# One core of a Trainium2 chip: a new hand-written order for the first layer norm and transform of a spectral block with a gated feed-forward, with its loads cut differently

## The chip, the cores and the metric

The kernel runs on one core of a Trainium2 chip. The time is device microseconds of one execution, taken as the median of several runs; smaller is better. Besides the time there is one profiled execution, whose trace shows every instruction of the engines: PE (TensorE matmul) with PEld (its weight loads), DVE (VectorE), ACT (ScalarE), POOL (GpSimd) and SP (SyncE, which here only issues DMAs). Times inside the trace are microseconds from the start of its span.

## The reference

```python
def A(x, w_r, w_i):                      # spectral filter over (2048 tokens, 576 features)
    X = rfft2(x.astype(float32)) * (w_r + 1j * w_i)
    return irfft2(X, s=(2048, 576)).astype(bfloat16)
def B(x, w_gate, w_up, w_down):          # 576 -> 4608 -> 576
    return (gelu(x @ w_gate) * (x @ w_up)) @ w_down
h   = x + A(layernorm(x))
out = h + B(layernorm(h))
```

All inputs are bfloat16, with 2048 tokens of 576 features, and the layer norms have no parameters.

## The kernel before

The 2048 tokens are held as 16 tiles of 128 partitions (token 16p + c is partition p of tile c), each 576 wide, in `XO`. The kernel has four stages, all in one program whose instructions are recorded in order and given to the engines as one queue each; an engine runs its queue strictly in order, and semaphore waits are derived from what each operation reads and writes.

**Front (L484 to L585).** For each tile a mean and variance is formed: on DVE by two `bn_stats` of half a tile each (L496) and one `bn_aggr` (L505), or, for the three tiles named by a `Q` token, on ACT by a sum (`S`, L488) and a sum of squares (`Q`, L492), after which POOL squares the mean (`m`, L499) and DVE forms the variance (L508). The 16 tiles go in six groups, of 2, 2, 3, 3, 3 and 3 tiles. For each group ACT takes a square root (`q`, L512), DVE a reciprocal (`c`, L517), and the transform table `ATB` is scaled by it into `ATS` (`x`: on POOL one instruction for a group, L522; on DVE one for each tile, L527). POOL also negates a part of the tiles into `XN` (`n`, L569) and copies 64 tail columns of each tile into it (`t`, L574). The token transform `M` (`a_mm`, L553) of a group is five positions of 2 matmuls for each tile; each position writes a PSUM bank of its own, and the banks go round in eights, so that a position of a later group waits until an earlier position's bank has been emptied. Emptying is the eviction `E` (L564, on ACT or DVE) into `U`. Evictions whose number appears in an `F` token are split: `E` moves the half of the columns that the first half of the next stage reads, and `F` moves the rest later. `k` puts matmuls on zeros into the PE queue.

The order of all of this is written out by hand in the string `SEQ1` (L25): each word is an operation, its group, tile or eviction number, and, with A, D or P behind it, the engine. `M3`, for example, is the transform of group 3, and `E18D` eviction number 18 on DVE. Eviction number n belongs to group n // 5.

**D stage (SEQF, about 20 to 43.6 us).** For 16 frequency groups: feature transform D (L642), B (L662), multiplication T by the filter on DVE (L675), V (L683), with evictions on ACT and DVE (L608). The filter lies in `WS`. SP loads it from HBM in many small pieces (`w_up`, `w_down`, `w_zero`); two of the `w_down` pieces are issued by POOL. Then `WS` is duplicated on the other partitions by `dup_w`: piece 0 by two POOL instructions (L732, behind the last `x`) and two DVE instructions (L730), and pieces 1 to 3 by DMAs that POOL issues. T of group i reads the duplicate 0 for i below 5, 1 from 5, 2 from 8, and 3 from 12 on.

**Inverse transform (SEQ)** with the residual add and the second layer norm, to about 55.5 us; loads of the first gate and up weights are held back on SP until given matmuls. **Feed-forward**: four blocks of 512 tokens, each 36 gate and up products (L946) and the down product (L1046, L1058).

The load order of the front is `LORD` (L26): `x4-8` is one DMA with tiles 4 to 7 of the input, and `a4-8` one with those tiles' tables. They go out on SP in that order, ahead of the tables `FT` and `BT`, the filter pieces and `VT`.

Of the kernel before, what the change touches and what calls it, by code (L numbers as in the profile page):

```python
# [7 lines left out]
ALU = mybir.AluOpType  # L8
# [12 lines left out]
NPRE = 8  # L21
PARTS = ((0, 256), (256, 512))
GROUPS = ((0, 2), (2, 4), (4, 7), (7, 10), (10, 13), (13, 16))
SEQ1 = """B0 b0 S3 B2 Q3 n0 B1 b1 b2 n1 t0 m3P t2 v0 v1 n2 t1 q0 c0 k14 x0D q1 M0 E0A S4 m4P c1 x1D n3 E2A k104 b5 t3 b7 Q4 E1A M1 E7A B5 B6 E8A b6 B7 v2 q2 B11 E5A B8 c2 x2P E3A E9A b8 b9 B9 v3 E6A n4 B12 Q13 E4A k206 M2 b10 q3 c3 b11 S13 x3P E11A B10 t4 b12 v4 E10A B14 m13P E14A M3 q4 c4 x4P E12A E13A t5 b14 E15A b15 B15 v5 E16A E18D E17A q5 M4 E20A E19A E23A c5 x5D n5 E24A F24D F23D E21A M5 E25A E26D E22A E28D E27A E29D F25A F29D F26A F27A F28A F22A""".split()
LORD = "x0-2 x2-4 a0-4 x4-8 a4-8 x8-12 x12-16 a8-16".split()  # L25
SPLIT = tuple(int(w[1:-1]) for w in SEQ1 if w[0] == "F")  # L26
ACT_TILES = tuple(int(w[1:]) for w in SEQ1 if w[0] == "Q")
SEQF = """D2 D0 d2 D1 d0 d1 B2 D5 B0 d5 T2 D3 B1 d3 D4 T0 T1 B5 d4 D8 B3 d8 D7 T3 B4 d7 V0 D6 v0 V1 T5 d6 v1 R0 V2 r0 v2 T4 B6 D9 B8 T6 V3 d9 D11 v3 d11 B7 D10 B9 d10 V6 V4 T7 v6 v4 V5 B10 v5 R1 D12 T8 r1 d12 B11 T9 V7 D14 v7 T10 d14 D13 B12 d13 D15 T11 V9 T12 d15 v9 V8 B13 v8 R2 r2 T13 B14 T14 B15 V12 V10 v12 v10 V13 V11 T15 v13 V14 v11 v14 V15 R3 v15 r3""".split()
# [9 lines left out]
def _np_bf16(a):  # L38
    npdt = mybir.dt.np(BF16)
    return np.ascontiguousarray(np.asarray(a, dtype=np.float32).astype(npdt))  # L40
# [291 lines left out]
def _build(nc, A_x, A_w_r, A_w_i, B_w_gate, B_w_up, B_w_down, out):  # L332
    P = Prog(nc)
    T = build_tables()
    dram = {n: nc.inline_tensor(_np_bf16(T[n]), name="c_" + n.lower()) for n in T}
    PE, DVE, ACT, SP, POOL = "pe", "dve", "act", "sp", "pool"
# [4 lines left out]
    XO = sb.alloc("XO", [128, NT, D], BF16)  # L341
# [19 lines left out]
    XN = sb.alloc("XN", [128, NT, 448], BF16)  # L361
# [27 lines left out]
    BT = sb.alloc("BT", [128, 2, 2, 128], BF16)  # L389
    VT = sb.alloc("VT", [128, 6, 2, 128], BF16)  # L390
# [32 lines left out]
    def bank(b, p0=0, p1=128, c0=0, c1=512):  # L423
        return PS[p0:p1, b * 512 + c0:b * 512 + c1]
# [18 lines left out]

    for i, w in enumerate(LORD):
        (x_load if w[0] == "x" else atb_load)(i, int(w[1:].split("-")[0]), int(w.split("-")[1]))
    P.dma(SP, FT[:, :, :].rearrange("p a b -> p (a b)"), dram["FTAB"][:, :], "ft", w=["FT"])
    P.dma(SP, BT[:, 0, :, :].rearrange("p b c -> p (b c)"), dram["BTAB"][:, 0:256], "bt", w=["BT"])

    def w_up(pl, hf):
        g0, g1 = ((0, 9), (9, 16))[hf]  # L450
# [5 lines left out]
    def w_down(pl, hf, sls=(0, 1, 2, 3), eng=SP, sem=""):  # L456
        g0, g1 = ((1, 9), (9, 16))[hf]
        src = (A_w_r, A_w_i)[pl].tensor
        for sl in sls:
            p0 = 64 * (sl // 2) + 32  # L460
            P.dma(eng, WS[p0 + sl % 2:p0 + 32:2, sl // 2, pl, g0:g1, :], bass.AP(src, (64 + 16 * (3 - sl) + 16 - g0) * K2, [[128 * K2, 16], [-K2, g1 - g0], [1, K2]]),
                  f"w{pl}{hf}{sem}", w=[("W", hf, pl, 2 + sl)])

    def w_zero(pl):
        for jp in range(2):
            P.dma(SP, WS[64 * jp + 32:64 * jp + 64, jp, pl, 0, :], bass.AP((A_w_r, A_w_i)[pl].tensor, (64 + 32 * jp) * K2, [[128 * K2, 16], [(-16 if jp else 48) * K2, 2], [1, K2]]),
                  f"wz{pl}", w=[("W", 2, pl, jp)])

    for pl in (1, 0):
        w_up(pl, 0)  # L470
        w_down(pl, 0)
    P.dma(SP, VT[:, 0, :, :].rearrange("p b c -> p (b c)"), dram["VTAB"][:, 0:256], "vt", w=["VT"])
    for pl in (1, 0):
        w_up(pl, 1)
        w_down(pl, 1, (0, 1, 2, 3) if pl else (0, 1))
    for pl in (1, 0):
        w_zero(pl)
    P.dma(SP, VT[:, 1, :, :].rearrange("p b c -> p (b c)"), dram["VTAB"][:, 256:512], "vt1", w=["VT1"])
    P.dma(SP, BT[:, 1, :, :].rearrange("p b c -> p (b c)"), dram["BTAB"][:, 256:512], "bt1", w=["BT1"])
    GORD = list(range(1, NG)) + [0]  # L480
    wkeys = [[("W", hf, pl, h) for pl in range(2) for h in range(6 if hf < 2 else 2)] for hf in range(3)]

# [47 lines left out]
    AORD = (1, 0, 3, 2, 4)  # L530

    def a_bank(i, k):
        return (5 * i + AORD.index(k) + ABASE) % 8

    def idle_mm(a):
        b = a_bank(a // 100, AORD[0])
        for _ in range(a % 100):
            P.op(PE, lambda t: t.matmul(bank(b), ZD[:, 0:128], ZD[:, :], start=True, stop=True), r=["ZD"], w=[("PS", b)])  # L538

# [24 lines left out]
        fn = (lambda v: v.tensor_copy(dst, src)) if eng == DVE else (lambda a: a.activation(dst, src, ACTF.Copy))  # L564
        P.op(eng, fn, r=[("PS", b)] + ([("EV", n)] if late else []), w=[("U", i, k, h) for h in hs] + ([] if late else [("EV", n)]))

    def x_neg(i):
        c0, c1 = GROUPS[i]
        P.op(POOL, lambda g: g.tensor_scalar(XN[:, c0:c1, 0:256], XO[:, c0:c1, 288:544], -1.0, 1.0, op0=ALU.mult, op1=ALU.mult),  # L569
             r=[("X", c) for c in range(c0, c1)], w=[("XN", c) for c in range(c0, c1)])  # L570

    def x_tail(i):
        c0, c1 = GROUPS[i]
        P.op(POOL, lambda g: g.tensor_scalar(XN[:, c0:c1, 320:384].rearrange("p c (a e) -> p c a e", a=2),  # L574
                                             XO[:, c0:c1, :].rearrange("p c (a e) -> p c a e", a=2)[:, :, :, 256:288], 1.0, 1.0, op0=ALU.mult, op1=ALU.mult),
             r=[("X", c) for c in range(c0, c1)], w=[("XT", c) for c in range(c0, c1)])

    P.op(DVE, lambda v: v.memset(XN[:, :, 256:448].rearrange("p c (a e) -> p c a e", e=64)[:, :, 0::2, :], 0.0), w=["XZ"])

    ENG = {"A": ACT, "D": DVE, "P": POOL}  # L580
    RUN1 = {"k": idle_mm, "S": act_sum, "Q": act_sq, "B": lambda c: ln1_half(c, 0), "b": lambda c: ln1_half(c, 1), "v": ln1_var, "q": ln1_sqrt, "c": ln1_rs, "M": a_mm, "x": ln1_scale, "E": a_ev, "F": lambda n, eng: a_ev(n, eng, True), "n": x_neg, "t": x_tail, "m": act_mean2}
    P.op(ACT, lambda a: a.activation(SA[:, 0, 0:1], EPT[:, 0:1], ACTF.Sqrt), r=["EPT"], w=[("SA0", 0)])
    for w in SEQ1:
        a = w[1:]
# [9 lines left out]
    for t, w in enumerate(SEQF):  # L594
        k, i = w[0], w[1:].rstrip("abc")
        if k in "DBVR":
            b = min((b for b in used if b not in busy), key=lambda b: used[b])
# [4 lines left out]
        elif k in "dvr":  # L602
            b = FB[k.upper(), int(i)]
# [117 lines left out]
    def dup_w(k, jp, pl=slice(0, 2), eng=None):  # L721
        a, b = 64 * jp, 64 - 64 * jp
        n = ("Wd", k, jp, pl.start)
        for g0, g1 in (((1, 6),), ((6, 9),), ((9, 13),), ((13, 16), (0, 1)))[k]:
            dst, src = (WS[q:q + 64, jp, pl, g0:g1, :].rearrange("p a g k -> p a (g k)")[:, :, 1:] for q in (b, a))
            r = [x for x in (wkeys[1] if g0 > 8 else wkeys[0] if g0 else wkeys[0] + wkeys[2]) if pl.start <= x[2] < pl.stop]
            if eng is None:
                op = P.dma(POOL, dst, src, f"wd{k}{jp}", r=r, w=[(*n, g0)])
            elif eng == DVE:
                P.op(DVE, lambda v: v.tensor_copy(dst, src), r=r, w=[(*n, g0)])  # L730
            else:
                P.op(POOL, lambda v: v.tensor_scalar(dst, src, 1.0, 1.0, op0=ALU.mult, op1=ALU.mult), r=r + [("ATS", NT - 1)], w=[(*n, g0)])  # L732
        return op if eng is None else None

    for jp in range(2):
        dup_w(0, jp, slice(1, 2), POOL)
        dup_w(0, jp, slice(0, 1), DVE)
    for jp in range(2):
        dup_w(1, jp)
    w_down(0, 1, (2, 3), POOL, "p")  # L740
    c = 0
    while c < NT:
        c1 = c + 1
# [5 lines left out]
        c = c1  # L749
# [34 lines left out]
    for w in SEQF:  # L784
        i = int(w[1:].rstrip("abc"))
# [26 lines left out]
    for t, w in enumerate(SEQ):  # L812
        k, i = w[0], int(w[1:].rstrip("ADSP"))
        if k in "INu":
            b = min((b for b in range(2 * ing, 4) if b not in held), key=lambda b: last[b])
# [3 lines left out]
        elif k in "ioUEae":  # L819
            b = SLOT[{"i": "I", "o": "N", "U": "u", "E": "I", "a": "N", "e": "u"}[k], i] // 2  # L820
# [145 lines left out]
    for w in SEQ:  # L966
        a = w[1:]
# [132 lines left out]
def bass_sequential_preLN__spectral_gfnet__geglu_ffn__prompt_kernel(  # L1100
    nc, A_x, A_w_r, A_w_i, B_x, B_w_gate, B_w_up, B_w_down, out
):
    _build(nc, A_x, A_w_r, A_w_i, B_w_gate, B_w_up, B_w_down, out)
# [28 lines left out]
```

## Time and profile before

| what | us |
|---|---|
| median of 3 runs (lowest, highest) | 486.07 (485.85, 486.44) |
| the profiled execution's own time | 485.97 |
| its span in the trace | 484.2 |
| PE busy | 477.5 (99%) |
| DVE, ACT, POOL busy | 183.3, 146.3, 52.2 |
| first transform matmul (M0), first D matmul | 7.08, 19.91 |
| end of the D stage's chain, first gate matmul | 43.6, 55.47 |
| granted TensorE clock | 1.00 in every stretch asked for |

The span is the trace's first to last instruction; the profiled execution took 1.77 us more than that. A timeline row gives the start, the duration, the engine, the line, the operation, and `out<-in` with the number of instructions in it; a duration of several instructions runs from the first one's start to the last one's end, and instructions of one engine overlap a little, so the distance from start to start ("pitch") is what one costs in a row of them.

### The profile page before, as it was taken

How to read it: one execution, taken by the hardware profiler on the slowest of the kernel's cores; microseconds unless marked ns; L12 is line 12 of the kernel's file. 1: busy time of each engine (PE TensorE's matmuls, PEld its weight loads, DVE VectorE, ACT ScalarE, POOL GpSimd, SP SyncE). 2: the span in 40 equal slices, each digit the busy share in tenths (PEclk: the TensorE clock that was granted, in tenths of full speed). 3: DMA queues.
4: the chain of work that ended last, by engine and by line, in shares of the span. 5: the costliest groups of instructions: out<-in, count | busy, mean ns of one | idle time of the engine just before them, and what ended most of it. 6: DMA issues, size and time to landing. Idle time of an engine off the chain costs nothing.

```text
span 484.2 us, 12895 instructions
## 1 busy us (share of the span) xinstructions
PE 477.5 (99%) x5875; PEld 304.4 (63%) x5876; DVE 183.3 (38%) x366; ACT 146.3 (30%) x295; POOL 52.2 (11%) x88
## 2 busy tenths in 40 slices
PE   8999999999999999999999999999999999999998
PEld 4877765555588744444688644444788544445884
DVE  7898755665500144333200234333101233333011
ACT  6998753434300032233100132223100133223000
POOL 6873317010120000000000000000000000000000
DMA  8865889941430001000000011000000000000000
GB/s 283 215 142 160 251 279 282 374 109 27 173 100 27 26 15 23 20 1 0 3 14 15 26 24 23 13 1 1 3 14 27 14 1 1 0 1 1 3 26 26
DMA packets 28582, 33.19 MB, mean 69 GB/s; under 512 B 12640, under 2 KB 21872, under 8 KB 28528
## 3 DMA queue, kind: packets, MB, share of 16 engines
q1 hardware_dynamic: 24864, 19.87, 14.3%
q0 software_dynamic: 3664, 12.50, 8.1%
q8 instruction: 46, 0.75, 0.7%
q14 instruction: 8, 0.07, 0.1%
HBM read 26.21 MB, written 2.36 MB: 59 GB/s over the span
## 4 chain that ended last, share of the span: by engine, by line
PE 95%; DMA 1%; DVE 1%; POOL 1%; SPq 0%; issue 0%; POOLq 0%; DVEq 0%
PE PS L946 58%; PE PS L1046 27%; PE PS L642 2%; PE PS L1058 2%; PE PS L683 2%; DMA XO<-in_A_x_dram 1%; PE PS L553 1%; PE PS L662 1%; PE PS L837 1%; PE PS L996 1%; DVE XO L860 1%; SPq L242 0%; PE PS L1013 0%; PE PS L854 0%; POOL XN L569 0%
## 5 line engine op out<-in xcount | busy, mean ns | idle before, releaser
L946 PE MATMUL PS<-HT,WG 64*128 64x512 bf16 (+1 forms) x2142 | 233.5, 373 | 0.1
L946 PEld LDWEIGHTS PS<-HT,WG 64*128 64x128 bf16 x2142 | 116.1, 94 | 104.4 <-DVE AT L955 0.2
L954 ACT ACTIVATE GL<-PS 128x512 bf16<-128x512 f32 x144 | 85.7, 596 | 281.7 <-PE PS L946 281.7
L955 DVE TENSOR_TENSOR AT<-GL,PS 128x512 bf16<-128x512 bf16 x144 | 98.8, 687 | 166.0 <-ACT GL L954 166.0
L1046 PE MATMUL PS<-WD,AT 64*128 64x288 bf16 x2160 | 133.0, 283 | 0.0
L1046 PEld LDWEIGHTS PS<-WD,AT 64*128 64x128 bf16 x2160 | 114.3, 94 | 18.7
L1033 DVE TENSOR_TENSOR OS<-PS,XO 128x288 bf16<-128x288 f32 (+2 forms) x32 | 13.2, 452 | 125.5 <-PE PS L1046 118.0
L946 PE MATMUL PS<-HT,WGX 64*128 64x512 bf16 x486 | 53.5, 376 | 0.0
L946 PEld LDWEIGHTS PS<-HT,WGX 64*128 64x128 bf16 x486 | 25.7, 94 | 26.7
L863 ACT ACTIVATE OS<-XO,NM 128x576 bf16<-128x576 bf16 x15 | 11.6, 773 | 11.4 <-DVE XO L1017 11.4
L642 PE MATMUL PS<-FT,U 64*128 64x288 bf16 x160 | 13.3, 283 | 0.0
L675 DVE TENSOR_TENSOR TP<-YS,WS 128x1024 bf16<-128x1024 bf16 x16 | 11.0, 686 | 0.4 <-PE PS L683 0.2
L564 ACT ACTIVATE U<-PS 128x384 bf16<-128x384 f32 (+2 forms) x31 | 10.5, 427 | 1.2 <-PE PS L553 1.1
L496 DVE BATCH_NORM_STATS2 ST<-XO 128x6 f32<-128x288 bf16 x26 | 10.0, 441 | 1.8 <-DMA XO<-in_A_x_dram 1.8
L242 POOL DMA_DIRECT2D WG<-in_B_w_gate_dram x9 | 6.1, 679 | 35.5 <-DMA WG<-in_B_w_gate_dram 32.1
L683 PE MATMUL PS<-VT,TP 64*128 64x128 bf16 x256 | 9.9, 217 | 0.0
L553 PE MATMUL PS<-ATS,XO 128*128 128x128 bf16 x96 | 8.2, 220 | 1.5 <-POOL ATS L522 0.8
L242 POOL DMA_DIRECT2D WD<-in_B_w_down_dram x9 | 6.7, 756 | 22.9 <-PE PS L1013 22.9
L608 ACT ACTIVATE CUS<-PS 128x576 bf16<-128x576 f32 x14 | 9.1, 656 | 0.4 <-PE PS L642 0.2
L1058 PE MATMUL PS<-WD,AT 128*128 128x448 bf16 (+1 forms) x72 | 9.0, 286 | 0.0
L538 PE MATMUL PS<-ZD 128*128 128x512 bf16 x23 | 7.5, 484 | 1.5 <-POOL ZD L431 1.5
L608 ACT ACTIVATE YS<-PS 128x576 bf16<-128x576 f32 x14 | 8.8, 653 | 0.1
(88 smaller groups left out, 231.3 us busy)
## 6 DMA issues: line engine op xcount, KB each, us to landing
WD<-in_B_w_down_dram POOLq DMA_DIRECT2D x9, 576.0 KB, 13.0
WG<-in_B_w_up_dram SPq DMA_DIRECT2D x6, 576.0 KB, 6.6
WG<-in_B_w_gate_dram POOLq DMA_DIRECT2D x6, 576.0 KB, 6.2
out_dram<-OS SPq DMA_DIRECT2D x30, 72.0 KB, 1.7
XO<-in_A_x_dram SPq DMA_DIRECT2D x3, 576.0 KB, 7.1
WGX<-in_B_w_up_dram SPq DMA_DIRECT2D x2, 576.0 KB, 4.5
WGX<-in_B_w_gate_dram POOLq DMA_DIRECT2D x2, 576.0 KB, 5.8
HT<-HN SPq DMA_TRANSPOSE x60, 2.4
```

What stands on the lines that cost most here:

```text
L242: fn = lambda e: e.dma_start(out_ap, in_ap)
L553: P.op(PE, lambda t, b=b, lhs=lhs, p0=p0, p1=p1, s=s, e=e, o=o, c=c: t.matmul(bank(b, p0, p1, o, o + 128), lhs, ATS[:, c, :], start=s, sto ...
L608: fn = (lambda v: v.tensor_copy(dst, src)) if eng == DVE else (lambda a: a.activation(dst, src, ACTF.Copy))
L642: return P.op(PE, lambda t: t.matmul(bank(b0 + o, 0, 128, 0, 2 * HK), U[64 * h:64 * h + 64, us, 2 * i:2 * i + 2, :, :], FT[64 * h:64 * h + ...
L683: return P.op(PE, lambda t: t.matmul(bank(b0 + o, 0, 128, 128 * c, 128 * c + 128), TP[64 * h:64 * h + 64, z, o, t_, c:256:2], VT[64 * h:64 ...
L863: P.op(ACT, lambda a, c=c, out=out: a.activation(out, XO[:, c, 0:D], ACTF.Square, bias=NM[:, c:c + 1], accum_out=SB2[:, 1, c:c + 1]), r=[( ...
L946: op = P.op(PE, lambda t, h0=h0, kt=kt, wt=wt, b=b, s=(not second and j == 0), e=(second and j == n - 1): t.matmul(bank(b, 0, 128, c0, c1) ...
L954: P.op(ACT, lambda a: a.activation(GL[:, s2, :], bank(b0), ACTF.Gelu_apprx_tanh), r=[("PS", b0)], w=[("GL", s2)])
L955: P.op(DVE, lambda v: v.tensor_tensor(AT[:, f, :], GL[:, s2, :], bank(b0 + 1), op=ALU.mult), r=[("GL", s2), ("PS", b0 + 1)], w=[("AT", f)])
L1033: P.op(DVE, lambda v: v.tensor_tensor(OS[:, p % 2, d0:d1], bank(b, 0, 128, 0, d1 - d0), XO[:, c, d0:d1], op=ALU.add), r=[("PS", b), ("X", ...
L1046: e[h] = P.op(PE, lambda t, f=f, h=h, r0=r0, j=j: t.matmul(bank(b0 + h, 0, 128, 0, 288), AT[r0:r0 + 64, f, 128 * p:128 * p + 128], WD[r0:r ...
L1058: P.op(PE, lambda t, b=b, d0=d0, d1=d1, f=f, j=j: t.matmul(bank(b, 0, 128, 0, d1 - d0), AT[:, f, 128 * p:128 * p + 128], WD[:, f, d0:d1], ...
```

## The change

- `LORD`: the tiles 4 to 11 come in four pieces of two tiles where two pieces of four stood; the tables 4 to 15 come as one piece, between tiles 8-12's second half and tiles 12-16, where they came as two pieces, `a4-8` after tiles 4-8 and `a8-16` last of all. SP issues nine loads where it issued eight.
- `BT` and the first third of `VT` are loaded whole in one DMA each; the two late DMAs with their second parts are gone from SP.
- `SEQ1` is another order. The tiles with statistics on ACT are 2, 7 and 10 (before 3, 4 and 13). The scaling `x` of groups 0 and 1 is on POOL (before DVE). The tail copies `t2`, `t4` and `t5` are on DVE (before POOL). Four evictions are split (22, 27, 28, 29; before 22 to 29). DVE has the evictions 18, 20, 24 and 25, the first halves 27 and the second halves 27 and 22. The matmuls on zeros between the groups are 8 ahead of M2 (before 4 ahead of M1 and 6 ahead of M2).
- The two filter pieces on POOL stand ahead of `dup_w(0)` in its queue, where they stood behind `dup_w(1)`.
- `idle_mm`, `x_neg` and `x_tail` take one more argument.

```diff
-SEQ1 = """B0 b0 S3 B2 Q3 n0 B1 b1 b2 n1 t0 m3P t2 v0 v1 n2 t1 q0 c0 k14 x0D q1 M0 E0A S4 m4P c1 x1D n3 E2A k104 b5 t3 b7 Q4 E1A M1 E7A B5 B6 E8A b6 B7 v2 q2 B11 E5A B8 c2 x2P E3A E9A b8 b9 B9 v3 E6A n4 B12 Q13 E4A k206 M2 b10 q3 c3 b11 S13 x3P E11A B10 t4 b12 v4 E10A B14 m13P E14A M3 q4 c4 x4P E12A E13A t5 b14 E15A b15 B15 v5 E16A E18D E17A q5 M4 E20A E19A E23A c5 x5D n5 E24A F24D F23D E21A M5 E25A E26D E22A E28D E27A E29D F25A F29D F26A F27A F28A F22A""".split()
-LORD = "x0-2 x2-4 a0-4 x4-8 a4-8 x8-12 x12-16 a8-16".split()
+SEQ1 = """b1 n0 S2 b0 B1 Q2 t1 B0 v0 b3 n1 m2P B3 q0 c0 t0 v1 q1 x0P B5 k14 M0 c1 x1P b4 E0A E1A n2 M1 B4 t3 b5 S7 E2A Q7 b6 n3 B6 v2 q2 B9 S10 E5A b8 B8 c2 E3A b9 m7P v3 E4A q3 t2D Q10 b11 B11 c3 x2P b12 m10P B12 E6A E7A E8A x3P v4 k208 M2 E9A B13 q4 B14 E10A E11A E14A M3 c4 E12A n4 E13A B15 b14 b13 b15 v5 E15A q5 E18D x4P E16A t4D c5 M4 t5D x5D E17A E21A E19A n5 E22A E20D E24D E23A M5 E25D E26A E27D E28A E29A F27D F28A F29A F22D""".split()
+LORD = "x0-2 x2-4 a0-4 x4-6 x6-8 x8-10 x10-12 a4-16 x12-16".split()
...
-    P.dma(SP, BT[:, 0, :, :]..., dram["BTAB"][:, 0:256], "bt", w=["BT"])
+    P.dma(SP, BT[:, :, :, :]..., dram["BTAB"][:, :], "bt", w=["BT", "BT1"])
...
-    P.dma(SP, VT[:, 0, :, :]..., dram["VTAB"][:, 0:256], "vt", w=["VT"])
+    P.dma(SP, VT[:, 0:2, :, :]..., dram["VTAB"][:, 0:512], "vt", w=["VT", "VT1"])
...
-    P.dma(SP, VT[:, 1, :, :]..., dram["VTAB"][:, 256:512], "vt1", w=["VT1"])
-    P.dma(SP, BT[:, 1, :, :]..., dram["BTAB"][:, 256:512], "bt1", w=["BT1"])
...
+    w_down(0, 1, (2, 3), POOL, "p")
     for jp in range(2):
         dup_w(0, jp, slice(1, 2), POOL)
         dup_w(0, jp, slice(0, 1), DVE)
     for jp in range(2):
         dup_w(1, jp)
-    w_down(0, 1, (2, 3), POOL, "p")
```

More of the change, by code (lines that the diff above doesn't have):

```diff
@@ L446, in _build @@
     P.dma(SP, FT[:, :, :].rearrange("p a b -> p (a b)"), dram["FTAB"][:, :], "ft", w=["FT"])
-    P.dma(SP, BT[:, 0, :, :].rearrange("p b c -> p (b c)"), dram["BTAB"][:, 0:256], "bt", w=["BT"])
+    P.dma(SP, BT[:, :, :, :].rearrange("p a b c -> p (a b c)"), dram["BTAB"][:, :], "bt", w=["BT", "BT1"])
     def w_up(pl, hf):
@@ L471, in _build @@
         w_down(pl, 0)
-    P.dma(SP, VT[:, 0, :, :].rearrange("p b c -> p (b c)"), dram["VTAB"][:, 0:256], "vt", w=["VT"])
+    P.dma(SP, VT[:, 0:2, :, :].rearrange("p a b c -> p (a b c)"), dram["VTAB"][:, 0:512], "vt", w=["VT", "VT1"])
     for pl in (1, 0):
@@ L477, in _build @@
         w_zero(pl)
-    P.dma(SP, VT[:, 1, :, :].rearrange("p b c -> p (b c)"), dram["VTAB"][:, 256:512], "vt1", w=["VT1"])
-    P.dma(SP, BT[:, 1, :, :].rearrange("p b c -> p (b c)"), dram["BTAB"][:, 256:512], "bt1", w=["BT1"])
     GORD = list(range(1, NG)) + [0]
@@ L535, in idle_mm @@
     def idle_mm(a):
-        b = a_bank(a // 100, AORD[0])
+        b = a_bank(a // 100 % 10, AORD[a // 1000])
         for _ in range(a % 100):
@@ L565, in a_ev, with x_neg, x_tail @@
         P.op(eng, fn, r=[("PS", b)] + ([("EV", n)] if late else []), w=[("U", i, k, h) for h in hs] + ([] if late else [("EV", n)]))
-    def x_neg(i):
+    def x_neg(i, eng=POOL):
         c0, c1 = GROUPS[i]
-        P.op(POOL, lambda g: g.tensor_scalar(XN[:, c0:c1, 0:256], XO[:, c0:c1, 288:544], -1.0, 1.0, op0=ALU.mult, op1=ALU.mult),
+        P.op(eng, lambda g: g.tensor_scalar(XN[:, c0:c1, 0:256], XO[:, c0:c1, 288:544], -1.0, 1.0, op0=ALU.mult, op1=ALU.mult),
              r=[("X", c) for c in range(c0, c1)], w=[("XN", c) for c in range(c0, c1)])
-    def x_tail(i):
+    def x_tail(i, eng=POOL):
         c0, c1 = GROUPS[i]
-        P.op(POOL, lambda g: g.tensor_scalar(XN[:, c0:c1, 320:384].rearrange("p c (a e) -> p c a e", a=2),
+        P.op(eng, lambda g: g.tensor_scalar(XN[:, c0:c1, 320:384].rearrange("p c (a e) -> p c a e", a=2),
                                              XO[:, c0:c1, :].rearrange("p c (a e) -> p c a e", a=2)[:, :, :, 256:288], 1.0, 1.0, op0=ALU.mult, op1=ALU.mult),
```

## The prediction

> **What bounds the kernel now.** I read the chain of work that ended last, then its pieces in order of time, then the timeline of each engine to 28 us, then busy time by stretch.
>
> ```profile
> PE 95%; DMA 1%; DVE 1%; POOL 1%; SPq 0%; issue 0%; POOLq 0%; DVEq 0%
> ```
>
> ```profile
> 3.06 7.08 DMA XO<-in_A_x_dram
> ...
> 14.53 1.85 PE PS L553 x30
> 16.47 3.51 PE PS L553 x60
> 19.98 2.01 PE PS L642 x30
> ...
> 55.47 6.31 PE PS L946 x92
> ```
>
> From 55.47 us on PE runs without a break and nothing in the change touches it. What can move is when the D stage begins (19.91) and how much of that reaches 55.47. Before 19.91 stand M4 and M5 (3.51 for both). M5 waits for its scaled table, x5D on DVE:
>
> ```profile
> 3.69 2.26 DVE L496 BATCH_NORM_STATS2 ST<-XO 128x6 f32<-128x288 bf16 x6 [1.77 <-DMA XO<-in_A_x_dram]
> ...
> 17.43 0.62 DVE L527 TENSOR_SCALAR ATS<-ATB,RS 128x128 bf16<-128x128 bf16 x3
> 18.70 2.06 DVE L564 CAST U<-PS 128x192 bf16<-128x192 f32 x6 [0.66 <-ACT U L564]
> 20.80 1.35 DVE L730 COPY WS<-WS 64x1444 bf16<-64x1444 bf16 x2
> ```
>
> x5D ends at 18.05, M5's first matmul starts at 18.09, and M5 takes 1.82. DVE works from 3.69 to 18.05, 14.36 us. I can account for it by pitches: 26 half-tile statistics at 0.364 (six are 2.26, the last lasting 0.44) are 9.46; 13 aggregates at 0.085 and 3 variances at 0.14 are 1.53; six reciprocals at 0.08 are 0.48; E18 0.50; x0D and x1D 0.71; x5D 0.62. That is 13.3. Waits for ACT's square roots are 0.63 (0.20, 0.20, 0.23); scalings that follow directly on their reciprocal lose 0.44 (0.19 to 0.27 from start to start instead of 0.08). **DVE's own queue sets the start of M5.** ACT is as full behind it:
>
> ```profile
> 17.03 3.81 ACT L564 ACTIVATE U<-PS 128x384 bf16<-128x384 f32 x13
> 18.18 2.86 POOL L732 TENSOR_SCALAR WS<-WS 64x1444 bf16<-64x1444 bf16 x2 [0.51 <-DVE ATS L527]
> ```
>
> **DVE's queue after.** It loses x0D, x1D (0.71) and gets t2D, t4D, t5D. A tail copy of 192 columns is not shown on DVE. Bounds: the reciprocal's pitch 0.08, and POOL's own 0.35 for the same copy; I take 0.20, nearest to the table scaling (0.165 from start to start for 128 columns). Three are 0.60 (0.24 to 1.05). Work is then 13.2, and the 0.44 falls away: x0, x1 are gone from DVE and t5D stands between c5 and x5D. From 3.69 that gives 16.9 plus waits. Waits, in queue order:
> - c0 waits for q0, which stands behind S2 and Q2 on ACT; in the rows those two run 4.40 to 5.84, so the root ends at 6.1. DVE gets there at 6.05: 0.15.
> - B5 waits for tiles 4-6, at 6.50. Tiles 4-8 landed at 7.6 (issued 2.11, landing 5.5) and a0-4 at 5.64; half of the bytes gives 6.65: 0.15.
> - b12 waits for tiles 12-16. DVE reaches it at 12.1. Before, these tiles landed at 11.5 (issued 3.5, the longest landing 8.0) and a8-16, last, at 12.4. After, the same 2816 KB are issued up to and with tiles 12-16, so they land by 12.4; the one table piece of 384 KB should save some (128 KB of tables took 7.6 to 8.38, 0.78, where input tiles move 576 KB in 1.37): 12.1 to 12.4, wait 0 to 0.3.
>
> So x5D ends at 17.2 to 17.5; I take 17.4, 0.65 before 18.05.
>
> **The other queues up to M5.**
> - PE: M0 needs x0P. POOL's scaling of 256 columns is not shown; 0.55 to 0.83, nearest the 0.83 of 384 columns cut by a third. c0 ends at 6.3, x0P at 6.95, M0 starts at 7.0 (7.08 before). M1 follows at 8.1 without the 4 zero matmuls between (8.91 before). Neither binds: DVE does.
> - POOL: x2P needs c2 (10.35) and the table a4-16, which by bytes lands at 10.75; it ends at 11.65 and M2 starts at 11.7 (12.54 before). x3P stands behind m10P, which needs Q10 (ACT, 12.3): 12.75 to 13.6, M3 at 13.65 (14.53 before). n4 and x4P at 0.83 each with 0.17 between end at 15.5: M4 at 15.55 (16.47 before). M4 ends near 17.3, before x5D. The cover of the three groups is 0.1 to 0.9; gone, they cost one for one.
> - ACT: one full eviction more (0.40 pitch), five halves fewer (0.24 each): 0.8 less, so that it ends at 20.0 instead of 20.84. M4 and M5 need banks emptied by E12 to E17, E19 and E21: by 0.40 each from q4 (13.65) they are empty at 15.25 to 17.85, each just ahead of its position; E16 at 16.65 against 16.9 is the closest. This cover is 0.1 to 0.3.
> - DVE behind x5D: E20, E24, E25 at 0.50, E27, F27, F22 at 0.34: ends at 19.9 (20.76 before), and dup (1.35) at 21.3. The D stage's first pair needs E25 (18.9) and E26 (ACT, 18.9), the next E27 (19.25) and E28: all about when M5 ends.
>
> **Sum.** M5 from 17.5 to 19.3; D starts 0.6 earlier.
>
> **What does that become?** Order and banks of the D stage are the same, and PE, ACT, DVE enter 0.6, 0.8, 0.8 earlier. What stands on other clocks: POOL's dup 0 waits for x5D and the filter's first half; the moved pieces take 2 issues (1.13) after n5, to about 17.7, then dup 2.86 ends near 20.5 (21.04 before), and dup 1's DMAs go out 0.5 earlier; T5 at 27.57 needs them, which 4.8 after issue land by 26.6. The filter's second half no longer waits for those two pieces (POOL idle 1.77 until 27.89), so dups 2 and 3 go out earlier, and SP's table loads, held by the last dup until 36.13, too. No wait in the D stage is for these, so I count this as nothing; it is cover. The two DMAs taken from SP (1.0 us of issue, 25.06 to 26.11) are followed by a wait until 29.20: nothing. The extra load on SP delays the filter issues by 0.5, and 128 KB more come ahead of the second half's; the DMAs are full until 18 us and the first half is read by DVE only at 19.9: nothing, with 1 us of cover. Further on, weight loads are held on matmuls and move along.
>
> Sum: 485.97 (profiled execution) less 0.6 is 485.4. The median of the runs, 486.07, stands 0.10 above that execution, inside their spread. 0.2% is 0.97 us, about what a measurement here can tell from no change; I expect less than that.
>
> **Rivals.**
> - **More of it: 484.9.** DVE and ACT are 95% busy through the D stage, and they are freed 0.8 earlier, not 0.6. With a4-16 and tiles 12-16 landing at 12.1, tail copies at 0.08 (0.36 less) and the 0.15 at B5 gone, x5D ends at 16.9, and ACT's chain (E17 at 17.05) is next: M5 at 17.1, 1.0 earlier, and 0.1 more if half of what the evictions are ahead counts. For: the D stage's chain hops between PE and its evictions. Against: E16, E17 then bind.
> - **Slower: tiles 12-16 late, 487.2.** They are issued last now, behind 384 KB of tables. If these tables move as a4-8 did (0.78 for 128 KB) they take 2.4 after 9.8, and tiles 12-16 come 1.4 later, at 13.6; if they also share the DMA engines with what is issued behind them, they land with FT, whose row is 4.6 plus 9.5, 14.1. DVE's queue is in order: b12 holds B13 to B15, v5, t4D, x5D. A landing at 14.1 is 2.0 of wait, x5D at 19.25, 1.2 later than before, and M4 waits with it. Above a landing of 12.9 the change loses, above 13.9 by over 0.2%. For: DMA busy share 1.04 to 1.12 from 10 to 18 us. Against: a8-16 (256 KB) took only 0.9, and pieces landed in order of issue.
> - **DVE and POOL in each other's way: 486.2.** t4D, t5D, x5D now run beside n5 and POOL's DMA issues (15.6 to 17.7). One row shows the effect: a POOL instruction on one column took 0.64 beside DVE's product, 0.18 without.
>
> ```profile
> 25.10 0.69 DVE L675 TENSOR_TENSOR TP<-YS,WS 128x1024 bf16<-128x1024 bf16 x1
> ...
> 25.20 0.64 POOL L747 TENSOR_SCALAR NM<-SA 128x1 f32<-128x1 f32 x1
> ```
>
> If a DVE copy waits for n5 (rest 0.25) and one issue (0.6), 0.85 eats the gain: +0.25. Against: x5D's first copy, beside n5 in the trace, took 0.30 instead of 0.24. The Trainium skill, SBUF — State Buffer, section "Who interferes with whom", speaks for the full price: a VectorE copy or tensor_scalar in a two-port mode and a GpSimd instruction shut each other out for the whole instruction, and so do a VectorE one with two SBUF inputs and a GpSimd one that reads SBUF. The slow 0.64 row agrees; the 0.30 row doesn't.
> - **The gain is taken back: 486.0.** Something in the D stage that comes at a fixed time (a filter piece, dup 1) becomes the wait. Against: the 1 us of cover.
>
> **Chances.** Forecast (485.1 to 485.8) 0.50; more 0.26; slower 0.11; in each other's way 0.07; taken back 0.06. Faster by over 0.2% is 0.26, slower 0.11, within 0.63. Range: the tail copies (0.24 to 1.05) and landings (0 to 0.3) alone give 484.9 to 486.0; with part of both outer rivals, 484.7 to 486.5.
>
> **What would show it.** Right: x5D ends at 17.2 to 17.5 with no DMA wait over 0.3 ahead of b12; first L642 matmul at 19.3; the first L946 matmul at 54.9; a DVE row L574 of 0.2 to 0.3. Wrong: a DVE wait for XO near 12 us, x5D's row well over 0.62, M4 or M5 waiting for ACT's U, or a D start that is earlier with the first L946 where it was. The forecast fails if any wait in the D stage exceeds its row of before by the 0.6.

## The result, and the profile after

The changed kernel takes 485.49 us (median of 18 runs, 484.82 to 486.45); the kernel before takes 486.45 (18 runs, 485.85 to 487.65). The ratio of all runs is 0.9978, 95% interval 0.9971 to 0.9985: 1.07 us faster (0.7 to 1.4); the medians alone differ by 0.96. The three runs shown ahead of the prediction (486.07) lay 0.4 under the median of the 18. The profiled execution of the changed kernel took 486.04, in the upper half of its 18; that of before (485.97) was among its shortest. So the two profiles, both with a span of 484.2, show no difference at the end, and the reader has to see where a gain was made and where this one execution lost it.

The chain that ended last, after; line numbers are two lower than before from the loads on:

```profile
PE 91%; SPq 3%; DMA 2%; DVE 2%; ACT 1%; issue 0%; DVEq 0%
```

Its pieces in order of time (start, duration, what):

```profile
13.12 0.60 SPq L242
13.77 6.59 DMA WS<-in_A_w_r_dram
21.50 0.63 DVE CUS L606
...
41.02 3.68 DMA VR<-RB
45.16 1.08 PE PS L835 x14
...
55.54 6.31 PE PS L944 x92
```

The front has left the chain. In its place stand SP's issues, one after the other from 0.73, up to a filter piece that lands at 20.36. Later come the row moves, the DMAs that bring rearranged rows into `VR`, which land at 44.70; the place where the inverse transform's second products (`DT` with `VR`) need these rows is called the join below. The gate matmuls begin at 55.54 (55.47 before).

DVE's timeline after:

```profile
3.73 1.54 DVE L494 BATCH_NORM_STATS2 ST<-XO 128x6 f32<-128x288 bf16 x4 [1.81 <-DMA XO<-in_A_x_dram]
...
16.30 0.22 DVE L572 TENSOR_SCALAR XN<-XO 128x192 bf16<-128x192 bf16 x1
16.44 0.57 DVE L525 TENSOR_SCALAR ATS<-ATB,RS 128x128 bf16<-128x128 bf16 x3
16.93 2.40 DVE L562 CAST U<-PS 128x384 bf16<-128x384 f32 x6
20.38 1.07 DVE L728 COPY WS<-WS 64x1444 bf16<-64x1444 bf16 x2 [1.05 <-DMA WS<-in_A_w_r_dram]
```

x5D ends at 17.01 (18.05 before), and the D stage starts at 18.86 (19.91): 1.05 earlier, not 0.6. A tail copy takes 0.24, 0.16 from start to start. Then DVE is ready at 19.33 and waits 1.05 for the filter. POOL, DVE and PE show what follows:

```profile
20.64 1.54 POOL L242 DMA_DIRECT2D WS<-WS  x2 [0.34 <-DMA WS<-in_A_w_r_dram]
...
27.89 3.59 POOL L242 DMA_DIRECT2D WS<-WS  x6 [2.55 <-DMA WS<-in_A_w_r_dram]
```

```profile
27.51 0.70 DVE L673 TENSOR_TENSOR TP<-YS,WS 128x1024 bf16<-128x1024 bf16 x1 [0.95 <-PE PS L698]
```

```profile
45.16 0.35 PE L835 MATMUL PS<-DT,VR 64*128 64x288 bf16 x2 [0.65 <-DMA VR<-RB]
```

Duplicate 1 goes out 0.35 earlier only, and DVE stands idle for 0.95 ahead of T5, until 27.51 (27.57 before). The row puts this down to PE, but in the trace duplicate 1 lands at 27.43, just as those products end, and six other profiles name the duplicate at this place. Duplicates 2 and 3 go out when they did, and what is left (0.26 at 43.36, where the inverse transform starts) goes in the wait for `VR`. The kernel before stood at the same place:

```profile
45.10 0.34 PE L837 MATMUL PS<-DT,VR 64*128 64x288 bf16 x2 [0.33 <-issue]
```

Its last row landed at 44.64, 0.46 ahead of this product; after, it is 44.70 and 45.16. So the join was a wait of 0.3 in the profile of before already, and a D stage that is earlier helps in full only if the rows come earlier too.

### The profile page after: what moved, and what is told of

Read it like the earlier page. It is cut to its first block, busy times and chain, and to the rows that moved or that the text cites. A ratio compares the mean times of both kernels' runs of the same rounds, so it can differ in the third digit from the quotient of the medians.

```text
span 484.2 us, 12888 instructions
## 1 busy us (share of the span) xinstructions
PE 477.1 (99%) x5874; PEld 279.1 (58%) x5874; DVE 182.8 (38%) x365; ACT 145.4 (30%) x291; POOL 53.2 (11%) x88
## 4 chain that ended last, share of the span: by engine, by line
PE 91%; SPq 3%; DMA 2%; DVE 2%; ACT 1%; issue 0%; DVEq 0%
PE PS L944 58%; PE PS L1044 27%; SPq L242 3%; PE PS L1056 2%; DMA WS<-in_A_w_r_dram 1%; PE PS L640 1%; DMA VR<-RB 1%; PE PS L994 1%; DVE XO L858 1%; PE PS L681 1%; ACT YS L606 1%; PE PS L835 0%; PE PS L660 0%; PE PS L1011 0%; PE PS L852 0%
## 5 line engine op out<-in xcount | busy, mean ns | idle before, releaser
L944 PEld LDWEIGHTS PS<-HT,WG 64*128 64x128 bf16 x2142 | 105.8, 94 | 114.5 <-DVE AT L953 0.2
L1044 PEld LDWEIGHTS PS<-WD,AT 64*128 64x128 bf16 x2160 | 102.5, 94 | 30.6
L944 PEld LDWEIGHTS PS<-HT,WGX 64*128 64x128 bf16 x486 | 23.0, 94 | 29.4
L562 ACT ACTIVATE U<-PS 128x384 bf16<-128x384 f32 (+2 forms) x27 | 9.4, 479 | 0.7 <-PE PS L551 0.7
L681 PEld LDWEIGHTS PS<-VT,TP 64*128 64x128 bf16 x256 | 8.0, 94 | 1.3
```

The lines of the kernel that those rows point to most:

```text
L681: return P.op(PE, lambda t: t.matmul(bank(b0 + o, 0, 128, 128 * c, 128 * c + 128), TP[64 * h:64 * h + 64, z, o, t_, c:256:2], VT[64 * h:64 ...
L944: op = P.op(PE, lambda t, h0=h0, kt=kt, wt=wt, b=b, s=(not second and j == 0), e=(second and j == n - 1): t.matmul(bank(b, 0, 128, c0, c1) ...
L1044: e[h] = P.op(PE, lambda t, f=f, h=h, r0=r0, j=j: t.matmul(bank(b0 + h, 0, 128, 0, 288), AT[r0:r0 + 64, f, 128 * p:128 * p + 128], WD[r0:r ...
```

## The experiments

All ratios are against the kernel before, run on the same chip, with five rounds each. The median of the kernel before lies between 486.24 and 486.45 on the chips used, so ratios are compared. A profile shows one execution, and its time is given where it lies at the edge of its kernel's runs.

**1. The changed kernel again.** No edit.

> The changed kernel once more, unaltered, to see how far a second profile of it agrees with the first. In the first, DVE's copy of the filter waited 1.05 us for a filter piece that landed at 20.36, and the gate matmuls began at 55.54 although the D stage had begun 1.05 us earlier than before. Theory F (the filter's landing takes the front's gain back, by an amount that varies with the landing): the landing differs from the first profile by up to 1 us, and the first gate matmul moves with it; the median over the rounds is 0.7 to 1.4 us under the kernel before. Rival J (a later join in the inverse transform, the rearranged rows that land at 44.7, holds the time whatever the front does): landing may move, the first gate matmul stays at 55.4 to 55.6 in every profile, and the time is within 0.3 us of before.

485.21, ratio 0.9974 (0.9963 to 0.9986). D starts at 18.75, the filter lands late again (DVE waits 1.23), T5 starts at 26.99, `VR`'s matmul waits 0.81, and the gate matmuls begin at 55.19. The front's gain repeats to 0.1 us; the end moves by 0.35 between two profiles of one kernel, and rival J, which held it at 55.4 to 55.6, falls. The landing at the copy hardly moved (20.42), so theory F names one of the waits, but not the one that differs.

**2. The filter pieces behind again.**

```diff
-    w_down(0, 1, (2, 3), POOL, "p")
     ...dup_w(0), dup_w(1)...
+    w_down(0, 1, (2, 3), POOL, "p")
```

> The changed kernel with one part undone: the two filter pieces on POOL again behind the first DMAs of the duplicate. Theory F, in the form that the DMA engines' traffic sets the landing: 126 KB in rows of 578 bytes are gone from the stretch 16 to 20 us, the filter's first half lands 0.4 to 1.0 us earlier than with the pieces in front (20.36), DVE's wait before its copy falls to under 0.7 us, and the time is the changed kernel's or up to 0.5 us less. Rival N (SP's issues one after the other set the landing, not the traffic): the landing stays within 0.2 us, and the time within 0.2 us of the changed kernel's. Rival P (the pieces in front are worth something, since the later duplicates wait for the second half): duplicates 2 and 3 go out later than 27.9, and the time rises by 0.2 to 0.6 us.

485.50, ratio 0.9983 (0.9972 to 0.9994), the changed kernel's within the intervals. In the profile the filter lands 0.9 earlier:

```profile
19.49 1.60 DVE L728 COPY WS<-WS 64x1444 bf16<-64x1444 bf16 x2 [0.20 <-DMA WS<-in_A_w_r_dram]
```

T5 starts at 26.39 without a wait, and the gate matmuls at 54.44, 1.03 ahead of before: in this execution, the shortest of its kernel (484.92), the front's gain arrives whole. SP's issue of that piece moved by 0.04 only, so rival N falls. That the pieces' traffic sets the landing, as theory F says, is not shown: `BT`, the load ahead of the filter, had already landed at 13.65 instead of 14.66, before POOL issued a piece at all (16.03). And with the pieces in front the half landed at 19.3 and 19.4 in experiments 3 and 10, with them behind at 20.7 in experiment 5. The median doesn't follow either. Duplicates 2 and 3 went out at 27.52, not later: rival P falls. Of the 0.9 only 0.4 is left behind the copy, which took 1.60 beside POOL's work instead of 1.07.

**3. Both tables in two parts again.** The edits to `BT` and `VT` undone, with the two late DMAs on SP.

> The changed kernel with the other DMA part undone: the first halves of the two tables first, their second parts in two late DMAs on SP. Ahead of the filter's first half stand 64 KB less and 0.24 us less of SP's issue. Theory F: the first half lands 0.2 to 0.5 us earlier and the time falls by up to 0.4 us; rival N gives 0.25 us of both; rival J no change of the time. The two late issues on SP cost nothing by all of them.

486.05, ratio 0.9995 (0.9986 to 1.0003): the gain is gone, against all three expectations. The copy no longer waits, but PE does, for the late part of `VT`, 0.88 at 28.34, where the changed kernel passes at 27.19.

**4. New order and new loads alone.** Edits 2 and 3 together.

> Only the new order of the front and the new order of the loads: both other DMA edits undone (pieces behind, tables in two parts). Theory F: the filter's first half lands by 19.6, DVE's copy waits under 0.3 us, the D stage keeps 0.8 to 1.05 us of the front's gain, and the time is 0.3 to 0.8 us under the changed kernel's, 484.7 to 485.2 on the scale where before is 486.4. Rival N: landing 20.1, time within 0.3 us of the changed kernel's. Rival J: no change against the changed kernel. Rival P: slower than the changed kernel by 0.2 to 0.6 us.

486.31, ratio 1.0001 (0.9992 to 1.0010). D starts at 18.76, 1.15 ahead of before, and nothing of it arrives, which no theory had:

```profile
28.15 0.29 PE L700 MATMUL PS<-VT,TR 64*128 64x128 bf16 x4 [1.17 <-DMA VT<-c_vtab]
```

With it V's products, queued behind on PE, are late, and so is everything that follows. In the profile of before PE reached this product at 28.07 with the table just there.

**5. Experiment 4 with VT whole.**

```diff
-    P.dma(SP, VT[:, 0, :, :]..., "vt", w=["VT"])
+    P.dma(SP, VT[:, 0:2, :, :]..., "vt", w=["VT", "VT1"])
```

> The kernel with the new order and loads alone, plus one more edit: the table VT is loaded with its second part at once, so that no late DMA brings that part; the other table stays in two parts and the filter pieces stay behind. In the kernel without this edit PE waited 1.17 us (28.15) for the late part, and the time was the one of before. Theory V (the late part of VT, which lands near 28 us whatever the front does, is what held the D stage; the other table and the pieces don't matter): the wait is gone, the first remaining-columns product of the D stage starts before 27.3, and the time is 0.6 to 1.2 us under the kernel before, within 0.3 us of the changed kernel. Rival F (the filter's first half is the hold): landing at 19.7 as without the edit, and no gain, within 0.3 us of before.

The wait for `VT` is gone (the product starts at 27.54), yet the time is 486.18, ratio 0.9995 (0.9983 to 1.0007), from 485.02 to 487.36. Theory V is right on the wait and misses the time. Its profile is of one of the slowest runs (487.34): the filter lands at 20.7, its second half later still (duplicates at 28.47), the four table loads behind them at 36.75, and the row moves last:

```profile
43.49 1.16 PE L836 MATMUL PS<-DT,V 64*128 64x288 bf16 x16 [0.38 <-DVE V L607]
46.47 0.34 PE L836 MATMUL PS<-DT,VR 64*128 64x288 bf16 x2 [1.83 <-DMA VR<-RB]
```

A second chain, of DMAs that begin with the filter's loads and not with the front's products, ends in this join. That it sets the typical time is not shown.

**6. The kernel before with both tables whole.** The edits of experiment 3, in the kernel before.

> The kernel before with one edit, both tables loaded whole and the two late DMAs gone; the old order of the front. In the profile of before PE reached the product that needs VT's second part at 28.07 with 0.2 us of wait, and not for this load. Theory V: the edit is worth nothing by itself, 0 to 0.3 us faster, since without the new front nothing reaches the table earlier. Rival W (the profile of before shows a lucky execution, its 485.97 against a median of 486.4; in most executions that load is late): 0.3 to 0.8 us faster. If the extra 128 KB ahead of the filter cost: up to 0.3 us slower.

486.70, ratio 1.0008 (0.9995 to 1.0022). Alone the edit is worth nothing, as theory V has it; rival W falls.

**7. Tail copies on POOL again.**

```diff
-... t2D ... t4D c5 M4 t5D x5D ...
+... t2 ... t4 c5 M4 t5 x5D ...
```

> The changed kernel with the three tail copies of groups 2, 4 and 5 on POOL again, the order otherwise the same. DVE loses three rows of 0.24 us (0.16 from start to start), POOL gets three of 0.35. On the chain of DVE, the scaling of the last group would end 0.2 us earlier; but on POOL the copies stand ahead of the scalings of groups 2 to 4 or ahead of the dup, so M4's last position and M5 wait. Theory D (what the front gained is the DVE queue's, and POOL has no room): D starts 0 to 0.4 us later than 18.86, the time 0 to 0.4 us over the changed kernel's. Rival: the copies on POOL are hidden, D starts 0.1 to 0.2 us earlier, the time is the same.

486.01, ratio 0.9990 (0.9982 to 0.9999): about half of the gain. D starts at 19.48, 0.6 later. Most of that is theory D's reason, above its 0.4: t2 stands ahead of x2P on POOL, x2P ends at 12.39 (11.77), M2 starts at 12.44 (11.83), and M4 ends 0.6 later. Something else comes on top: the three scalings of x5D take 1.23 together instead of 0.57, and the last of them 0.84:

```profile
16.73 0.83 POOL L567 TENSOR_SCALAR XN<-XO 128x768 bf16<-128x768 bf16 x1
16.77 0.84 DVE L525 TENSOR_SCALAR ATS<-ATB,RS 128x128 bf16<-128x128 bf16 x1
```

The last one ends 0.05 behind POOL's n5, which the tail copies had pushed to 16.73; in the changed kernel n5 is over at 16.08, before x5D starts. M5 waits 0.1 for it. So the tail copies on DVE save DVE no queue time: they let x2P go earlier on POOL, and they take n5 out of x5D's way, which would have cost 0.6 by itself had M4 not been as late.

**8. The kernel before with the pieces in front.** The edit of experiment 2 the other way.

> The kernel before with only the two filter pieces on POOL moved ahead of the duplicate. Theory V: no effect on the time, within 0.3 us, or slower by up to 0.5 us where POOL's dup 0 starts 1.1 us later (18.2 to 19.0) and dup 1 lands later than T5 wants it (27.6). Rival P (later duplicates waited for these pieces until 27.89, and gain from it): duplicates 2 and 3 go out 0.5 to 2 us earlier and the time falls by up to 0.4 us; against it speaks that with the changed kernel they still went out at 27.89, behind SP's own second-half pieces.

486.79, ratio 1.0012 (1.0003 to 1.0020): 0.6 slower. Duplicates 2 and 3 go out at 26.73 and gain nothing. In this execution, one of its longest (488.06), the inputs land late as well (x5D at 19.21), so the profile doesn't split the loss.

**9. The changed kernel with the old loads.**

```diff
-LORD = "x0-2 x2-4 a0-4 x4-6 x6-8 x8-10 x10-12 a4-16 x12-16".split()
+LORD = "x0-2 x2-4 a0-4 x4-8 a4-8 x8-12 x12-16 a8-16".split()
```

> The changed kernel with only the order and cut of its loads undone (tiles 4 to 11 in two pieces of four, tables in two pieces). In three profiles with the old loads and the old front, the longest landing of an input piece was 8.0, 8.5 and 9.5 us and the last scaling x5D ended at 18.05, 18.48 and 19.21; in five with the new loads and the new front (tail copies on DVE) 6.8 to 7.6 us and 16.9 to 17.4. Theory L (the cut of the loads is a good part of the front's gain, and most of its steadiness): DVE waits 0.4 to 1.5 us for input tiles, x5D ends 0.4 to 1.5 us later than 17.0, the time is 0.3 to 1.0 us over the changed kernel's. Rival O (the order of the engines' work is what gained; the loads come early enough either way): x5D within 0.3 us of 17.0 and the time within 0.3 us.

486.96, ratio 1.0008 (0.9997 to 1.0018): the whole gain gone. x5D ends at 18.31 and D starts at 20.26. The half of tile 5 that stands ahead of c1 in DVE's queue needs the piece with tiles 4 and 5, which now comes with 6 and 7. POOL's copy of group 3's tail columns needs tiles 8 and 9, which now come with 10 and 11:

```profile
7.93 0.46 DVE L494 BATCH_NORM_STATS2 ST<-XO 128x6 f32<-128x288 bf16 x1 [1.31 <-DMA XO<-in_A_x_dram]
```

```profile
10.54 0.35 POOL L572 TENSOR_SCALAR XN<-XO 128x192 bf16<-128x192 bf16 x1 [0.47 <-DMA XO<-in_A_x_dram]
```

The second wait is the one on the chain: from this copy POOL runs to x2P, which ends at 13.24 (11.77 in the changed kernel), M2 starts at 13.30, and PE has no wait over 0.2 from there to D. That is theory L, in the time at its upper end or beyond (some 1.5 us over the changed kernel by the ratios): the new order is built on the new pieces. The new pieces with the old order weren't tried.

**10. The changed kernel with VT in two parts.** The edit of experiment 5 the other way, in the changed kernel.

> The changed kernel with only VT in two parts again, the second part by a late DMA on SP; the other table whole, the pieces in front. Theory V (the late part of VT holds PE at the first remaining-columns product): a wait of 0.6 to 1.3 us for VT there, that product at 28.0 to 28.6 instead of 27.2, time 0.4 to 0.9 us over the changed kernel's. Rival B (it was the other table, since VT whole alone brought nothing in the time): a wait appears too, but the time stays within 0.25 us of the changed kernel's, because what follows waits for the rearranged rows anyway.

486.30, ratio 1.0000 (0.9989 to 1.0012). The wait is there, in an execution among the shortest of its kernel (485.69):

```profile
27.99 0.28 PE L699 MATMUL PS<-VT,TR 64*128 64x128 bf16 x4 [0.79 <-DMA VT<-c_vtab]
```

Theory V holds against rival B: this one late table is enough to undo the change, with more than the 0.9 that theory V allowed.

**11. The join rearranged.**

```diff
-LOADS = {"r0": "t", ...
+LOADS = {"r1": "t", ...
-                    k = (2 * j + t_) % 3 > 0
+                    k = (2 * j + t_) % 3 > 0 if q < 2 else t_
```

> The changed kernel with two edits at the join between the D stage and the inverse transform: SP's four table loads, which wait for the last duplicate, go behind the second set of row moves instead of ahead of it, and the third set of eight row moves is shared four and four between SP and POOL instead of three and five. Theory J (in an execution like the two profiled, the inverse transform waits 0.65 and 0.81 us for the last row moves, issued on SP as late as 41.0): the wait falls under 0.3 us, the inverse transform's second products start 0.3 to 0.8 us earlier, and the time falls by 0.2 to 0.6 us against the changed kernel. Rival F (what is lost is lost earlier, at the filter): the wait falls but the time moves by less than 0.2 us, or the table loads themselves come too late and a wait for them appears, 0.2 to 1 us slower.

486.02, ratio 1.0001 (0.9986 to 1.0016). The table loads go out 0.4 later and the row moves earlier, but these land no earlier: `VR`'s matmul waits 1.26 and starts at 45.23. Theory J in this form (SP's queue holds the row moves) falls.

**12. Pieces behind, and BT behind the filter's first half.**

```diff
-    P.dma(SP, BT[...], dram["BTAB"][:, :], "bt", ...)     # ahead of w_up, w_down
+    P.dma(SP, BT[...], dram["BTAB"][:, :], "bt", ...)     # just ahead of VT
```

> The changed kernel with the pieces on POOL behind again, as in the earlier run with only that undone (485.5, filter's first half at 19.49, DVE waiting 0.20 for it), and the whole table BT moved behind the filter's first half on SP. 128 KB and 0.74 us of issue fewer stand ahead of that half. Theory F (the landing of the filter's first half still costs): it lands 0.3 to 0.8 us earlier, DVE's copy follows its evictions without a wait, and the time is 0.1 to 0.4 us under the kernel with only the pieces undone, the fastest of all. Rival L (in this kernel what is left varies with the landings of later loads): no wait at the copy, the time within 0.2 us of 485.5. Rival T (the table comes too late for the first B product at 20.7): a wait of up to 1 us there and 0.2 to 0.8 us slower.

485.87, ratio 0.9995 (0.9984 to 1.0006). No wait at the copy, and no gain: theory F falls. Beside experiment 2 its profile is the clearest of all. The start of the inverse transform is the same to 0.01 us; then the products that need the moved rows start 0.74 apart. Experiment 2, then this one:

```profile
42.38 1.16 PE L835 MATMUL PS<-DT,V 64*128 64x288 bf16 x16 [0.38 <-DVE V L606]
44.06 0.34 PE L835 MATMUL PS<-DT,VR 64*128 64x288 bf16 x2 [0.52 <-DMA VR<-RB]
```

```profile
42.39 1.16 PE L835 MATMUL PS<-DT,V 64*128 64x288 bf16 x16 [0.38 <-DVE V L606]
44.80 0.34 PE L835 MATMUL PS<-DT,VR 64*128 64x288 bf16 x2 [1.25 <-DMA VR<-RB]
```

The gate matmuls follow at 54.44 and 55.18, and the spans are 483.1 and 483.9. So part of what is left over is decided at this join, and not alike in each execution: the two profiles of the changed kernel have 45.16 and 44.81 there.

## Why the prediction was right, and where its steps were not

**The total.** 485.4 was forecast, 485.49 measured, inside the range; the sign is right, and the gain of 1.07 lies a little beyond the 0.97 under which I expected it. The two closest numbers have two errors behind them that cancel: the base was taken 0.4 too low (three runs), and the gain 0.4 too small. That they cancel is luck. The profiled execution showed two of the forecast's own signs of being wrong: D earlier with the first gate matmul where it was, and a wait in the D stage (1.05 at the copy) over its row of before by more than 0.6. It went the way of the rival "the gain is taken back"; the median of the 18 did not.

**The front: right in direction, wrong in what sets M5.** "DVE's own queue sets the start of M5" failed. The end of M4 and the start of M5 on PE, before and after:

```profile
17.81 0.50 PE L553 MATMUL PS<-ATS,XN 128*128 128x128 bf16 x6
18.14 0.22 PE L553 MATMUL PS<-ATS,XO 128*128 128x128 bf16 x1
```

```profile
16.68 0.50 PE L551 MATMUL PS<-ATS,XN 128*128 128x128 bf16 x6
17.01 0.22 PE L551 MATMUL PS<-ATS,XO 128*128 128x128 bf16 x1
```

Six matmuls, 0.055 from start to start, and M5 follows at that distance: the 18.09 that was read as M5's first matmul is M4's last. It is so in thirteen of the fourteen profiles, with x5D over by 0.0 to 0.2 when M5 starts; only in experiment 7 does M5 wait (0.1) for x5D. What M4 hangs on stands in the chain of before, between its lines at 3.06 and 14.53:

```profile
10.22 0.84 POOL XN L569
11.13 0.36 POOL XN L574
11.65 0.83 POOL ATS L522
12.64 0.84 POOL XN L569
13.64 0.84 POOL ATS L522
```

An input piece (tiles 8 and on) lands at 10.14, POOL works from there to x2P and x3P, the scaled tables of M2 and M3, and M4 and M5 follow. After, tiles 8 and 9 landed at 7.96, x2P ended at 11.77, M2 started at 11.83 instead of 12.54, and M3 and M4 waited 0.45 less together: that is the 1.05, but for 0.1 that M4 and M5 took longer. DVE's queue came forward by as much (1.04) and would have held M5 had it not, but it was not what M5 waited for. The forecast had this path too ("M4 ends near 17.3, before x5D"; it ended at 17.0), and went by a DVE queue that it put 0.4 too late; that both moved alike is luck. In the term "from 3.69 that gives 16.9 plus waits" I added 0.5, and the execution shows under 0.2: tiles 4 to 6 came in time (6.41), tiles 12 to 16 held DVE for some 0.1 (12.06), and the tail copies cost 0.16 each, not 0.20. ACT's evictions ended at 19.74 (20.0 forecast). Rival "more of it" described the front better than the forecast did.

**"With 1 us of cover" failed.** I had the DMA engines full until 18 us and the filter's first half there long before 19.9. It landed at 20.36. In the trace of before its last piece had landed at 19.84, for a copy at 20.80: that is the 1 us, and the forecast's own 19.9 for DVE had used it up. After, SP issued this piece 0.66 later, it landed 0.5 later, and DVE was ready at 19.33. Busy time by stretch (last two columns: DMA busy share, GB/s), before and after:

```profile
14.00:18.00 4.00, 3.76 (x65) 3.45 (x63) 3.67 (x17) 3.94 (x12) 3.10 (x6) 1.00 1.08 276
18.00:22.00 4.00, 4.00 (x70) 3.51 (x69) 3.17 (x9) 3.78 (x13) 3.72 (x4) 1.00 0.59 130
```

```profile
14.00:18.00 4.00, 4.00 (x72) 3.79 (x70) 4.00 (x18) 4.00 (x13) 3.67 (x6) 1.00 1.12 222
18.00:22.00 4.00, 4.00 (x65) 2.92 (x62) 2.90 (x7) 3.78 (x10) 3.58 (x4) 1.00 0.99 193
```

At about the same busy share the engines moved 222 instead of 276 GB/s and stayed full to 22. The pieces in front don't explain this rate: in the other twelve profiles it is 219 to 241 GB/s, 230 in experiment 2 and 232 in experiment 6 with the pieces behind, so the 276 of before stands alone. What moves this landing by 1 us from one profile to the next (19.3 to 20.7 with the new order and loads) stays open.

**"Nothing" for the two DMAs taken from SP failed most.** I looked at what waits behind them on SP, and not at who reads what they bring. PE needs `VT`'s second part at 28.07 before, and with the new front at 27.2. Left late, it takes the whole gain (experiments 3, 4, 10); so the edit that I priced at zero is one without which the rest is worth nothing that was measured. (The cut of the input loads is another, experiment 9.) Before the change the table just came in time, which no wait in that trace betrays.

**"No wait in the D stage is for these" failed in part.** T5 waited 0.35 to 0.95 for duplicate 1 in seven profiles. What follows the last duplicate on SP, four table loads and then row moves, ends in the join, at 44.06 to 46.47, the one place where every profile with the new order and loads, `VT` whole and the tail copies on DVE waits (0.5 to 1.8). Why it varies stays open: experiment 11 shows that SP's order there is not it, and the table loads' own traffic (1.1 MB, issued just ahead of the last row moves) wasn't taken away.

**Rivals.** Late tiles 12 to 16 did not occur. DVE and POOL in each other's way did not occur in the changed kernel, but experiment 7 shows the mechanism at its full price, 0.6 on one scaling, of which 0.1 reached M5. I had read the 0.30 row as speaking against it, wrongly: that scaling ended 0.06 behind n5 too, whose rest was short. The Trainium skill, SBUF — State Buffer, section "Who interferes with whom" (such a pair shut each other out for the whole instruction), agrees with the 0.84 row.

**Open.** Experiments 2, 5 and 12 differ in `BT`'s cut and place alone, and their ratios (0.9983, 0.9995, 0.9995) overlap; whether it matters is not settled. Whether the pieces' place matters isn't either (0.9978 and 0.9983). No version measured is faster than the changed kernel.

## What to carry to other kernels

When an edit takes loads away from a queue, price it at the reader of those loads, as early as the other edits bring that reader forward; a load that just arrives in time shows no wait in the trace. Where a stage is brought forward, list every DMA that it will meet and how close each landing is; here the landings varied more from run to run than the engines did. Where PE runs group after group without a break, ask what started the first of them before naming the queue that feeds the last. And compare one profile with its kernel's median first: here two profiles with equal spans belong to kernels 1 us apart.

## What the runs showed of the hardware

- A table scaling on DVE that started 0.04 us behind a GpSimd instruction (n5) took 0.84 us instead of 0.24 and ended 0.05 behind it (experiment 7).
- The same front on the same input loads ended (x5D) at 18.05, 18.48 and 19.21 in three executions (before, experiments 6 and 8), in which the slowest input piece took 8.0, 8.5 and 9.5 us from issue to landing; with the new order and cut and the tail copies on DVE it ended at 16.9 to 17.4 in nine.
- SP's last row move of 8 KB took 3.0 to 4.3 us from issue to landing in the fourteen profiles, where the quickest row move took 1.8; why is not shown.
